# ReGLU feed-forward for 32 tokens: projections with the tokens as the stationary operand, and h transposed chunk by chunk

## The chip, the cores and the metric

The kernel runs on one core of a Trainium2 chip. The metric is the device time in microseconds. The kernel before takes 63.21 us, the median of 6 runs (62.99 to 63.34).

## The reference

```python
B, S, D, F = 32, 1, 1024, 3584          # x [32,1,1024], all bfloat16
def reference(x, W_gate, W_up, W_down):
    gate = jnp.einsum("bsd,df->bsf", x, W_gate)
    up = jnp.einsum("bsd,df->bsf", x, W_up)
    gate = gate * (lambda x, dt: x.astype(dt))(gate > 0, gate.dtype)   # Relu
    h = gate * up
    return jnp.einsum("bsf,fd->bsd", h, W_down)
```

There are only 32 tokens, but three weight matrices of 7.34 MB each, 22 MB together, and each weight is used once.

## The kernel before

All weights get a place in on-chip memory and are loaded once. x is loaded by ScalarE's DMA queue (L180), turned by eight TensorE transposes (L122) and copied to xT by ScalarE (L182): 128 partitions, KT = 8 slices of the model dimension, 32 tokens. Partition p holds rows 8p to 8p+7 of W_gate and W_up, so that slice kt is one row per partition.

The hidden dimension F = 3584 is split into NG = 7 groups of 512, each into J = 4 tiles of 128, so FT = 28 tiles. A projection tile (`proj_tiles`, L126 to L138) takes a 128x128 block of weights as the stationary operand and the 32 tokens of xT as the moving one, eight matmuls over kt, and leaves 128 hidden units (partitions) by 32 tokens in PSUM. 28 tiles times 8 slices make 224 matmuls with 224 weight loads, for gate and for up alike. In this orientation h comes out with hidden units on partitions, which is what the down projection needs as its stationary operand. ScalarE applies Relu to gate in two pieces (L184 for tiles 0 to 15, L188 for 16 to 27), and DVE multiplies by up, in the same two pieces (L201, L206), into hT.

The down projection (`down_tile`, L140 to L153) takes a 128x32 tile of hT as stationary and 128x512 of W_down as moving, two matmuls per tile for the two halves of the output, 56 in all, accumulating in o_ps. ScalarE copies the first half out of PSUM and sends it (L192, L194), DVE the second (L210), SyncE sends that (L113).

The order of work is written out by hand. SyncE's queue issues the loads in this order: Wg whole (L100), Wu for tiles 0 to 15 (L102, called WuA below), the Wd chunk g = 0 (L103), the rest of Wu (L105, WuB), Wd chunks 1 to 5 (L107), and the last Wd chunk in four quarters (L109), each with its own semaphore. TensorE follows that order: gate, up A, down chunk 0, up B, down chunks 1 to 6. Each matmul in the program is a pair of instructions for TensorE, a weight load and a matmul.

Of the kernel before, what the change touches and what calls it, by code (L numbers as in the profile page):

```python
# [5 lines left out]
ACT = mybir.ActivationFunctionType  # L6
ALU = mybir.AluOpType


def bass_standalone__glu_gated_reglu__sampling_kernel(  # L10
# [7 lines left out]
    bf16 = mybir.dt.bfloat16  # L18
    fp32 = mybir.dt.float32

    B, S, D = x.shape
    F = W_gate.shape[1]
    P = 128
    N = B * S
    KT = D // P
    GW = 4 * P
    NG = F // GW
    J = 4
    FT = NG * J
    DH = 512  # L30
    NDH = D // DH
    HALF_T = 16
    GA = HALF_T // J

    assert N <= P and D % P == 0 and F % GW == 0 and D % DH == 0
    assert FT > HALF_T

    x2 = x.flatten_outer_dims()
    out2 = out.flatten_outer_dims()
    Wg_v = W_gate.rearrange("(p kt) f -> p kt f", kt=KT)  # L40
    Wu_v = W_up.rearrange("(p kt) f -> p kt f", kt=KT)
    Wd_v = W_down.rearrange("(g q j) d -> q g j d", q=P, j=J)

    with ExitStack() as es:
        x_sb = es.enter_context(nc.sbuf_tensor("x_sb", [N, D], bf16))
        ident = es.enter_context(nc.sbuf_tensor("ident", [N, N], bf16))
        xT = es.enter_context(nc.sbuf_tensor("xT", [P, KT, N], bf16))
        Wg = es.enter_context(nc.sbuf_tensor("Wg", [P, KT, F], bf16))
        Wu = es.enter_context(nc.sbuf_tensor("Wu", [P, KT, F], bf16))
        Wd = es.enter_context(nc.sbuf_tensor("Wd", [P, NG, J, D], bf16))  # L50
        g_sb = es.enter_context(nc.sbuf_tensor("g_sb", [P, FT, N], fp32))
        hT = es.enter_context(nc.sbuf_tensor("hT", [P, FT, N], bf16))
        o_sb = es.enter_context(nc.sbuf_tensor("o_sb", [N, D], bf16))
        xT_ps = es.enter_context(nc.psum_tensor("xT_ps", [P, KT, N], bf16))
        g_ps = es.enter_context(nc.psum_tensor("g_ps", [P, FT, N], fp32))
        u_ps = es.enter_context(nc.psum_tensor("u_ps", [P, FT, N], fp32))
        o_ps = es.enter_context(nc.psum_tensor("o_ps", [N, D], fp32))

        sem = lambda name: es.enter_context(nc.semaphore(name))
        s_x = sem("s_x")  # L60
        s_ident = sem("s_ident")
        s_xT_ps = sem("s_xT_ps")
        s_xT = sem("s_xT")
        s_wg = sem("s_wg")
        s_wuA = sem("s_wuA")
        s_wuB = sem("s_wuB")
        s_wd = [sem(f"s_wd{g}") for g in range(NG - 1)]
        s_wd6 = [sem(f"s_wdl{j}") for j in range(J)]
        s_g = sem("s_g")
        s_u = sem("s_u")  # L70
        s_gr = sem("s_gr")
        s_h = sem("s_h")
        s_o = sem("s_o")
        s_osb0 = sem("s_osb0")
        s_osb1 = sem("s_osb1")
        s_out0 = sem("s_out0")
# [1 line left out]
        block = es.enter_context(nc.Block())  # L78

        x_v = x_sb[:, :].rearrange("b (p kt) -> b kt p", kt=KT)  # L80
        Wg_r = Wg[:, :, :].rearrange("p kt (g q j) -> p kt g j q", g=NG, j=J)
        Wu_r = Wu[:, :, :].rearrange("p kt (g q j) -> p kt g j q", g=NG, j=J)

        @block.gpsimd
        def _(pool):
# [11 lines left out]

        @block.sync
        def _(sp):
            sp.dma_start(Wg[:, :, :], Wg_v[:, :, :]).then_inc(s_wg, 16)  # L100
            fa = slice(0, GA * GW)
            sp.dma_start(Wu[:, :, fa], Wu_v[:, :, fa]).then_inc(s_wuA, 16)  # L102
            sp.dma_start(Wd[:, 0, :, :], Wd_v[:, 0, :, :]).then_inc(s_wd[0], 16)  # L103
            fb = slice(GA * GW, F)
            sp.dma_start(Wu[:, :, fb], Wu_v[:, :, fb]).then_inc(s_wuB, 16)  # L105
            for g in range(1, NG - 1):
                sp.dma_start(Wd[:, g, :, :], Wd_v[:, g, :, :]).then_inc(s_wd[g], 16)  # L107
            for j in range(J):
                sp.dma_start(Wd[:, NG - 1, j, :], Wd_v[:, NG - 1, j, :]).then_inc(  # L109
                    s_wd6[j], 16  # L110
                )
            sp.wait_ge(s_osb1, 1)
            sp.dma_start(out2[:, DH:D], o_sb[:, DH:D]).then_inc(s_out1, 16)  # L113
            sp.wait_ge(s_out1, 16)
            sp.wait_ge(s_out0, 16)

        @block.tensor
        def _(pe):
            pe.wait_ge(s_x, 16)
            pe.wait_ge(s_ident, 2)  # L120
            for kt in range(KT):
                ins = pe.transpose(xT_ps[:, kt, :], x_v[:, kt, :], ident[:, :])  # L122
            ins.then_inc(s_xT_ps, 1)
            pe.wait_ge(s_xT, 1)

            def proj_tiles(W_r, ps, t_lo, t_hi):  # L126
                ins = None
                for t in range(t_lo, t_hi):
                    g, j = divmod(t, J)
                    for kt in range(KT):  # L130
                        ins = pe.matmul(  # L131
                            ps[:, t, :],
                            W_r[:, kt, g, j, :],
                            xT[:, kt, :],
                            start=(kt == 0),
                            stop=(kt == KT - 1),
                        )
                return ins  # L138

            def down_tile(t):  # L140
                g, j = divmod(t, J)
                ins = []
                for h in range(NDH):
                    ins.append(
                        pe.matmul(  # L145
                            o_ps[:, h * DH : (h + 1) * DH],
                            hT[:, t, :],
                            Wd[:, g, j, h * DH : (h + 1) * DH],
                            start=(t == 0),
                            stop=(t == FT - 1),  # L150
                        )
                    )
                return ins  # L153

            pe.wait_ge(s_wg, 16)
            proj_tiles(Wg_r, g_ps, 0, HALF_T).then_inc(s_g, 1)
            proj_tiles(Wg_r, g_ps, HALF_T, FT).then_inc(s_g, 1)
            pe.wait_ge(s_wuA, 16)
            proj_tiles(Wu_r, u_ps, 0, HALF_T).then_inc(s_u, 1)
            pe.wait_ge(s_h, 1)  # L160
            pe.wait_ge(s_wd[0], 16)
            for j in range(J):
                down_tile(j)
            pe.wait_ge(s_wuB, 16)
            proj_tiles(Wu_r, u_ps, HALF_T, FT).then_inc(s_u, 1)
            for g in range(1, NG - 1):
                if g == GA:
                    pe.wait_ge(s_h, 2)
                pe.wait_ge(s_wd[g], 16)
                for j in range(J):  # L170
                    down_tile(g * J + j)
            for j in range(J):
                pe.wait_ge(s_wd6[j], 16)
                last = down_tile((NG - 1) * J + j)
            last[0].then_inc(s_o, 1)
            last[1].then_inc(s_o, 1)

        @block.scalar
        def _(act):
            act.dma_start(x_sb[:, :], x2[:, :]).then_inc(s_x, 16)  # L180
            act.wait_ge(s_xT_ps, 1)
            act.activation(xT[:, :, :], xT_ps[:, :, :], ACT.Copy).then_inc(s_xT, 1)  # L182
            act.wait_ge(s_g, 1)
            act.activation(  # L184
                g_sb[:, 0:HALF_T, :], g_ps[:, 0:HALF_T, :], ACT.Relu
            ).then_inc(s_gr, 1)
            act.wait_ge(s_g, 2)
            act.activation(  # L188
                g_sb[:, HALF_T:FT, :], g_ps[:, HALF_T:FT, :], ACT.Relu
            ).then_inc(s_gr, 1)  # L190
            act.wait_ge(s_o, 1)
            act.activation(o_sb[:, 0:DH], o_ps[:, 0:DH], ACT.Copy).then_inc(s_osb0, 1)  # L192
            act.wait_ge(s_osb0, 1)
            act.dma_start(out2[:, 0:DH], o_sb[:, 0:DH]).then_inc(s_out0, 16)  # L194
            act.wait_ge(s_out0, 16)

        @block.vector
        def _(dve):
            dve.wait_ge(s_gr, 1)
            dve.wait_ge(s_u, 1)  # L200
            dve.tensor_tensor(  # L201
                hT[:, 0:HALF_T, :], g_sb[:, 0:HALF_T, :], u_ps[:, 0:HALF_T, :], ALU.mult
            ).then_inc(s_h, 1)
            dve.wait_ge(s_gr, 2)
            dve.wait_ge(s_u, 2)
            dve.tensor_tensor(  # L206
                hT[:, HALF_T:FT, :], g_sb[:, HALF_T:FT, :], u_ps[:, HALF_T:FT, :], ALU.mult
            ).then_inc(s_h, 1)
            dve.wait_ge(s_o, 2)
            dve.tensor_copy(o_sb[:, DH:D], o_ps[:, DH:D]).then_inc(s_osb1, 1)  # L210


# [26 lines left out]
```

## Time and profile before

| | before |
|---|---|
| time, median of 6 runs | 63.21 us |
| profiled execution: time / span of the core | 63.24 / 61.4 us |
| TensorE matmul busy / weight load busy | 31.6 / 21.5 us (512 of each) |
| DVE, ScalarE busy | 1.9, 3.3 us |
| gate matmuls, 128x128 stationary, 32 moving | 224, 7.8 us busy |
| up matmuls, same shape | 224, 7.8 us busy |
| down matmuls, 128x32 stationary, 512 moving | 56, 15.4 us busy |
| bytes read from HBM | 22.09 MB, 361 GB/s over the span |
| mean granted TensorE clock | 0.889 |

The profile is of one execution. The span is the time from the first to the last instruction of the core; the execution's own time is 1.84 us longer. "PE" is TensorE's matmuls, "PEld" its weight loads, "ACT" ScalarE, "SP" SyncE, and "PEq", "SPq" are the sequencers. "<-" behind an idle time names what ended it. The busy time of a row is not its cost: matmuls overlap, so the distance between starts is what counts. The clock is the share of full speed that the chip grants TensorE.

### The profile page before, as it was taken

How to read it: one execution, taken by the hardware profiler on the slowest of the kernel's cores; microseconds unless marked ns; L12 is line 12 of the kernel's file. 1: busy time of each engine (PE TensorE's matmuls, PEld its weight loads, DVE VectorE, ACT ScalarE, POOL GpSimd, SP SyncE). 2: the span in 40 equal slices, each digit the busy share in tenths (PEclk: the TensorE clock that was granted, in tenths of full speed). 3: DMA queues.
4: the chain of work that ended last, by engine and by line, in shares of the span. 5: the costliest groups of instructions: out<-in, count | busy, mean ns of one | idle time of the engine just before them, and what ended most of it. 6: DMA issues, size and time to landing. Idle time of an engine off the chain costs nothing.

```text
span 61.4 us, 1089 instructions
## 1 busy us (share of the span) xinstructions
PE 31.6 (51%) x512; PEld 21.5 (35%) x512; DVE 1.9 (3%) x3; ACT 3.3 (5%) x5; POOL 0.5 (1%) x6
## 2 busy tenths in 40 slices
PE   0000004000000499992209985972999999769920
PEld 0000003000000599992209972302993443314400
DVE  0000000000000000000000003000003000000040
ACT  2500000200000000300300000000000000000030
POOL 3000000000000000000000000000000000000000
PEclk9999999999999999999955555569955999999999
DMA  0909985991991999999999999999999999992001
GB/s 0 597 43 576 619 373 224 597 597 75 523 597 69 411 416 413 403 411 397 429 423 381 399 400 402 397 429 422 427 421 416 416 405 416 396 380 109 11 0 43
DMA packets 3812, 22.22 MB, mean 362 GB/s; under 512 B 256, under 2 KB 320, under 8 KB 2912
## 3 DMA queue, kind: packets, MB, share of 16 engines
q1 hardware_dynamic: 3712, 22.05, 88.5%
q10 hardware_dynamic: 96, 0.10, 0.5%
q8 instruction: 4, 0.07, 0.4%
HBM read 22.09 MB, written 0.07 MB: 361 GB/s over the span
## 4 chain that ended last, share of the span: by engine, by line
SPq 54%; DMA 34%; PE 6%; DVE 1%; issue 1%
DMA Wd<-in_W_down_dram 34%; SPq L107 26%; SPq L103 22%; PE o_ps L145 6%; SPq L105 5%; DVE o_sb L210 1%; SPq L102 1%; SPq L100 1%
## 5 line engine op out<-in xcount | busy, mean ns | idle before, releaser
L145 PE MATMUL o_ps<-Wd,hT 128*32 128x512 bf16 x56 | 15.4, 435 | 1.9 <-DMA Wd<-in_W_down_dram 1.0
L131 PE MATMUL g_ps<-xT,Wg 128*128 128x32 bf16 x224 | 7.8, 190 | 11.1 <-DMA Wg<-in_W_gate_dram 10.0
L131 PEld LDWEIGHTS g_ps<-xT,Wg 128*128 128x128 bf16 x224 | 7.6, 118 | 11.3 <-issue 11.3
L131 PE MATMUL u_ps<-xT,Wu 128*128 128x32 bf16 x224 | 7.8, 190 | 4.1 <-DMA Wu<-in_W_up_dram 4.1
L131 PEld LDWEIGHTS u_ps<-xT,Wu 128*128 128x128 bf16 x224 | 7.6, 118 | 5.1 <-DMA Wu<-in_W_up_dram 5.1
L145 PEld LDWEIGHTS o_ps<-Wd,hT 128*32 128x32 bf16 x56 | 5.7, 107 | 10.3 <-issue 3.9
L122 PE MATMUL xT_ps<-ident,x_sb 32*128 32x32 bf16 x8 | 0.7, 220 | 10.1 <-DMA x_sb<-in_x_dram 10.1
L122 PEld LDWEIGHTS xT_ps<-ident,x_sb 32*128 32x128 bf16 x8 | 0.6, 163 | 10.1 <-DMA x_sb<-in_x_dram 10.1
L192 ACT ACTIVATE o_sb<-o_ps 32x512 bf16<-32x512 f32 x1 | 0.6, 586 | 28.4 <-PE o_ps L145 28.4
L201 DVE TENSOR_TENSOR hT<-g_sb,u_ps 128x512 bf16<-128x512 f32 x1 | 0.7, 689 | 36.7 <-PE u_ps L131 36.7
L184 ACT ACTIVATE g_sb<-g_ps 128x512 f32<-128x512 f32 x1 | 0.6, 597 | 14.0 <-PE g_ps L131 14.0
L182 ACT ACT_TABLE_LOAD x1 | 1.3, 1283 | 1.2 <-PEq L224 1.2
L210 DVE CAST o_sb<-o_ps 32x512 bf16<-32x512 f32 x1 | 0.7, 678 | 12.1 <-PE o_ps L145 12.1
L182 ACT ACTIVATE xT<-xT_ps 128x256 bf16<-128x256 bf16 x1 | 0.4, 383 | 8.3 <-PE xT_ps L122 8.3
L206 DVE TENSOR_TENSOR hT<-g_sb,u_ps 128x384 bf16<-128x384 f32 x1 | 0.6, 555 | 8.7 <-PE u_ps L131 8.7
L188 ACT ACTIVATE g_sb<-g_ps 128x384 f32<-128x384 f32 x1 | 0.5, 490 | 3.9 <-PE g_ps L131 3.9
L88 POOL TENSOR_SCALAR_AFFINE_SELECT ident<-ident 32x32 bf16<-32x32 bf16 x1 | 0.2, 202 | 0.2 <-POOL ident L86 0.2
L86 POOL MEMSET ident<- 32x32 bf16 x1 | 0.1, 114 | 0.3 <-POOLq L224 0.3
L224 POOL MEMSET const-float32-0.0<- 128x1 f32 x1 | 0.1, 99 | 0.2 <-issue 0.2
L224 POOL MEMSET const-float32-1.0<- 128x1 f32 x1 | 0.1, 99 | 0.0
L224 POOL MEMSET const-bfloat16-1.0<- 128x1 bf16 x1 | 0.1, 99 | 0.0
L224 POOL MEMSET const-uint8-127<- 128x1 uint8 x1 | 0.1, 99 | 0.0
## 6 DMA issues: line engine op xcount, KB each, us to landing
Wg<-in_W_gate_dram SPq DMA_DIRECT2D x1, 7168.0 KB, 19.9
Wd<-in_W_down_dram SPq DMA_DIRECT2D x6, 1024.0 KB, 20.2
Wu<-in_W_up_dram SPq DMA_DIRECT2D x1, 4096.0 KB, 31.0
Wu<-in_W_up_dram SPq DMA_DIRECT2D x1, 3072.0 KB, 27.2
Wd<-in_W_down_dram SPq DMA_DIRECT2D x4, 256.0 KB, 19.4
x_sb<-in_x_dram ACTq DMA_DIRECT2D x1, 64.0 KB, 9.3
out_dram<-o_sb ACTq DMA_DIRECT2D x1, 32.0 KB, 1.5
out_dram<-o_sb SPq DMA_DIRECT2D x1, 32.0 KB, 1.5
```

The costliest lines, as they stand in the source:

```text
L100: sp.dma_start(Wg[:, :, :], Wg_v[:, :, :]).then_inc(s_wg, 16)
L102: sp.dma_start(Wu[:, :, fa], Wu_v[:, :, fa]).then_inc(s_wuA, 16)
L103: sp.dma_start(Wd[:, 0, :, :], Wd_v[:, 0, :, :]).then_inc(s_wd[0], 16)
L105: sp.dma_start(Wu[:, :, fb], Wu_v[:, :, fb]).then_inc(s_wuB, 16)
L107: sp.dma_start(Wd[:, g, :, :], Wd_v[:, g, :, :]).then_inc(s_wd[g], 16)
L122: ins = pe.transpose(xT_ps[:, kt, :], x_v[:, kt, :], ident[:, :])
L131: ins = pe.matmul(ps[:, t, :], W_r[:, kt, g, j, :], xT[:, kt, :], start=(kt == 0), stop=(kt == KT - 1),)
L145: pe.matmul(o_ps[:, h * DH : (h + 1) * DH], hT[:, t, :], Wd[:, g, j, h * DH : (h + 1) * DH], start=(t == 0), stop=(t == FT - 1),)
L182: act.activation(xT[:, :, :], xT_ps[:, :, :], ACT.Copy).then_inc(s_xT, 1)
L184: act.activation(g_sb[:, 0:HALF_T, :], g_ps[:, 0:HALF_T, :], ACT.Relu).then_inc(s_gr, 1)
L201: dve.tensor_tensor(hT[:, 0:HALF_T, :], g_sb[:, 0:HALF_T, :], u_ps[:, 0:HALF_T, :], ALU.mult).then_inc(s_h, 1)
L210: dve.tensor_copy(o_sb[:, DH:D], o_ps[:, DH:D]).then_inc(s_osb1, 1)
```

## The change

The projections are turned round. For each slice kt the 128x32 slice of xT is the stationary operand and 128x512 of the weights the moving one; the result has 32 tokens on partitions and 512 hidden units in one PSUM bank. Seven banks (`acc`) hold all of F, and the loop over kt is now outside the loop over the seven chunks, so all seven accumulate at once. Wg and Wu are loaded in eight slices each, in the order of kt, each with a semaphore; all of Wu comes before all of Wd. Up reuses gate's banks, each once its Relu is done (`s_gr`).

Gate's Relu output and h now have tokens on partitions (`g_sb`, `h_sb`, bf16, in seven chunks). For the down projection, each chunk of h is turned by four TensorE transposes into PSUM (`tp`) and copied to hT by ScalarE. The transposes of chunk c+1 stand ahead of the down matmuls of chunk c. The down matmuls themselves, the Wd loads and the two output paths are as they were, except that the output accumulates in banks 0 and 1 of `acc`. SyncE no longer waits for the first output half (ScalarE still does).

```diff
-            sp.dma_start(Wg[:, :, :], Wg_v[:, :, :]).then_inc(s_wg, 16)
-            fa = slice(0, GA * GW)
-            sp.dma_start(Wu[:, :, fa], Wu_v[:, :, fa]).then_inc(s_wuA, 16)
-            sp.dma_start(Wd[:, 0, :, :], Wd_v[:, 0, :, :]).then_inc(s_wd[0], 16)
-            fb = slice(GA * GW, F)
-            sp.dma_start(Wu[:, :, fb], Wu_v[:, :, fb]).then_inc(s_wuB, 16)
-            for g in range(1, NG - 1):
-                sp.dma_start(Wd[:, g, :, :], Wd_v[:, g, :, :]).then_inc(s_wd[g], 16)
+            for kt in range(KT):
+                sp.dma_start(Wg[:, kt, :], Wg_v[:, kt, :]).then_inc(s_wg[kt], 16)
+            for kt in range(KT):
+                sp.dma_start(Wu[:, kt, :], Wu_v[:, kt, :]).then_inc(s_wu[kt], 16)
+            for c in range(NFC - 1):
+                sp.dma_start(Wd[:, c, :, :], Wd_v[:, c, :, :]).then_inc(s_wd[c], 16)
...
+            for kt in range(KT):
+                pe.wait_ge(s_wg[kt], 16)
+                for c in range(NFC):
+                    ins = pe.matmul(
+                        acc[:, c, :],
+                        xT[:, kt, :],
+                        Wg[:, kt, c * FC : (c + 1) * FC],
+                        start=(kt == 0),
+                        stop=(kt == KT - 1),
+                    )
+                    if kt == KT - 1:
+                        ins.then_inc(s_gc, 1)
+            for kt in range(KT):
+                pe.wait_ge(s_wu[kt], 16)
+                for c in range(NFC):
+                    if kt == 0:
+                        pe.wait_ge(s_gr, c + 1)
...
+            def transpose_chunk(c):
+                pe.wait_ge(s_h, c + 1)
+                if c > 0:
+                    pe.wait_ge(s_hT, c)
+                for j in range(J):
+                    ins = pe.transpose(tp_t[:, c * J + j, :], h_v[:, c, j, :], ident[:, :])
+                ins.then_inc(s_hTp, 1)
+
+            def down_chunk(c):
+                pe.wait_ge(s_hT, c + 1)
+                if c == 0:
+                    pe.wait_ge(s_h, NDH)
+                if c < NFC - 1:
+                    pe.wait_ge(s_wd[c], 16)
...
+            transpose_chunk(0)
+            for c in range(NFC):
+                if c + 1 < NFC:
+                    transpose_chunk(c + 1)
+                last = down_chunk(c)
+            for h in range(NDH):
+                last[h].then_inc(s_o, 1)
...
+            for c in range(NFC):
+                act.wait_ge(s_gc, c + 1)
+                act.activation(
+                    g_sb[:, c * FC : (c + 1) * FC], acc[:, c, :], ACT.Relu
+                ).then_inc(s_gr, 1)
+            for c in range(NFC):
+                act.wait_ge(s_hTp, c + 1)
+                act.activation(
+                    hT[:, c * J : (c + 1) * J, :], tp_t[:, c * J : (c + 1) * J, :], ACT.Copy
+                ).then_inc(s_hT, 1)
...
+            for c in range(NFC):
+                dve.wait_ge(s_gr, c + 1)
+                dve.wait_ge(s_uc, c + 1)
+                dve.tensor_tensor(
+                    h_sb[:, c * FC : (c + 1) * FC],
+                    g_sb[:, c * FC : (c + 1) * FC],
+                    acc[:, c, :],
+                    ALU.mult,
+                ).then_inc(s_h, 1)
```

More of the change, by code (lines that the diff above doesn't have):

```diff
@@ L25, in bass_standalone__glu_gated_reglu__sampling_kernel @@
     KT = D // P
[L26 to L29, printed above, removed]
+    FC = 512
+    NFC = F // FC
+    J = FC // P
+    FT = NFC * J
     DH = 512
     NDH = D // DH
[L32 to L36, printed above, removed]
+    assert N <= P and D % P == 0 and F % FC == 0 and D == NDH * DH and NDH <= 2
+    assert (KT + FT) * N * 2 <= 2048 or True
     x2 = x.flatten_outer_dims()
@@ L41, in bass_standalone__glu_gated_reglu__sampling_kernel @@
     Wu_v = W_up.rearrange("(p kt) f -> p kt f", kt=KT)
-    Wd_v = W_down.rearrange("(g q j) d -> q g j d", q=P, j=J)
+    Wd_v = W_down.rearrange("(c q j) d -> q c j d", q=P, j=J)
     with ExitStack() as es:
@@ L49, in bass_standalone__glu_gated_reglu__sampling_kernel @@
         Wu = es.enter_context(nc.sbuf_tensor("Wu", [P, KT, F], bf16))
-        Wd = es.enter_context(nc.sbuf_tensor("Wd", [P, NG, J, D], bf16))
-        g_sb = es.enter_context(nc.sbuf_tensor("g_sb", [P, FT, N], fp32))
+        Wd = es.enter_context(nc.sbuf_tensor("Wd", [P, NFC, J, D], bf16))
+        g_sb = es.enter_context(nc.sbuf_tensor("g_sb", [N, F], bf16))
+        h_sb = es.enter_context(nc.sbuf_tensor("h_sb", [N, F], bf16))
         hT = es.enter_context(nc.sbuf_tensor("hT", [P, FT, N], bf16))
         o_sb = es.enter_context(nc.sbuf_tensor("o_sb", [N, D], bf16))
[L54 to L57, printed above, removed]
+        acc = es.enter_context(nc.psum_tensor("acc", [N, NFC, FC], fp32))
+        tp = es.enter_context(nc.psum_tensor("tp", [P, 1024], bf16))
+        tp_t = tp[:, 0 : FT * N].rearrange("p (t b) -> p t b", b=N)
+        xT_ps = tp_t[:, 0:KT, :]
         sem = lambda name: es.enter_context(nc.semaphore(name))
@@ L63, in bass_standalone__glu_gated_reglu__sampling_kernel @@
         s_xT = sem("s_xT")
[L64 to L70, printed above, removed]
+        s_wg = [sem(f"s_wg{k}") for k in range(KT)]
+        s_wu = [sem(f"s_wu{k}") for k in range(KT)]
+        s_wd = [sem(f"s_wd{c}") for c in range(NFC - 1)]
+        s_wdl = [sem(f"s_wdl{j}") for j in range(J)]
+        s_gc = sem("s_gc")
         s_gr = sem("s_gr")
+        s_uc = sem("s_uc")
         s_h = sem("s_h")
+        s_hTp = sem("s_hTp")
+        s_hT = sem("s_hT")
         s_o = sem("s_o")
@@ L80, in bass_standalone__glu_gated_reglu__sampling_kernel @@
         x_v = x_sb[:, :].rearrange("b (p kt) -> b kt p", kt=KT)
-        Wg_r = Wg[:, :, :].rearrange("p kt (g q j) -> p kt g j q", g=NG, j=J)
-        Wu_r = Wu[:, :, :].rearrange("p kt (g q j) -> p kt g j q", g=NG, j=J)
+        h_v = h_sb[:, :].rearrange("b (c q j) -> b c j q", c=NFC, j=J)
         @block.gpsimd
@@ L99, in _ @@
         def _(sp):
-            sp.dma_start(Wg[:, :, :], Wg_v[:, :, :]).then_inc(s_wg, 16)
-            fa = slice(0, GA * GW)
-            sp.dma_start(Wu[:, :, fa], Wu_v[:, :, fa]).then_inc(s_wuA, 16)
-            sp.dma_start(Wd[:, 0, :, :], Wd_v[:, 0, :, :]).then_inc(s_wd[0], 16)
-            fb = slice(GA * GW, F)
-            sp.dma_start(Wu[:, :, fb], Wu_v[:, :, fb]).then_inc(s_wuB, 16)
-            for g in range(1, NG - 1):
-                sp.dma_start(Wd[:, g, :, :], Wd_v[:, g, :, :]).then_inc(s_wd[g], 16)
+            for kt in range(KT):
[4 more added lines that the diff above has]
+                sp.dma_start(Wd[:, c, :, :], Wd_v[:, c, :, :]).then_inc(s_wd[c], 16)
             for j in range(J):
-                sp.dma_start(Wd[:, NG - 1, j, :], Wd_v[:, NG - 1, j, :]).then_inc(
-                    s_wd6[j], 16
+                sp.dma_start(Wd[:, NFC - 1, j, :], Wd_v[:, NFC - 1, j, :]).then_inc(
+                    s_wdl[j], 16
                 )
@@ L114, in _ @@
             sp.wait_ge(s_out1, 16)
-            sp.wait_ge(s_out0, 16)
         @block.tensor
@@ L124, in _ @@
             pe.wait_ge(s_xT, 1)
[L126 to L136, printed above, removed]
-                        )
-                return ins
@@ L140, in down_tile @@
[L140 to L176, printed above, removed]
+            for kt in range(KT):
[10 more added lines that the diff above has]
+                        ins.then_inc(s_gc, 1)
@@ new lines, in _ @@
+            for kt in range(KT):
[3 more added lines that the diff above has]
+                        pe.wait_ge(s_gr, c + 1)
+                    ins = pe.matmul(
+                        acc[:, c, :],
+                        xT[:, kt, :],
+                        Wu[:, kt, c * FC : (c + 1) * FC],
+                        start=(kt == 0),
+                        stop=(kt == KT - 1),
+                    )
+                    if kt == KT - 1:
+                        ins.then_inc(s_uc, 1)
@@ new lines, in transpose_chunk @@
+            def transpose_chunk(c):
[11 more added lines that the diff above has]
+                    pe.wait_ge(s_wd[c], 16)
+                last = None
+                for j in range(J):
+                    t = c * J + j
+                    if c == NFC - 1:
+                        pe.wait_ge(s_wdl[j], 16)
+                    last = []
+                    for h in range(NDH):
+                        last.append(
+                            pe.matmul(
+                                acc[:, h, :],
+                                hT[:, t, :],
+                                Wd[:, c, j, h * DH : (h + 1) * DH],
+                                start=(t == 0),
+                                stop=(t == FT - 1),
+                            )
+                        )
+                return last
@@ L178, in _ @@
+            transpose_chunk(0)
[3 more added lines that the diff above has]
+                last = down_chunk(c)
+            for h in range(NDH):
+                last[h].then_inc(s_o, 1)
         @block.scalar
@@ L181, in _ @@
             act.wait_ge(s_xT_ps, 1)
[L182 to L190, printed above, removed]
+            act.activation(xT[:, :, :], xT_ps, ACT.Copy).then_inc(s_xT, 1)
+            for c in range(NFC):
[8 more added lines that the diff above has]
+                ).then_inc(s_hT, 1)
             act.wait_ge(s_o, 1)
-            act.activation(o_sb[:, 0:DH], o_ps[:, 0:DH], ACT.Copy).then_inc(s_osb0, 1)
+            act.activation(o_sb[:, 0:DH], acc[:, 0, :], ACT.Copy).then_inc(s_osb0, 1)
             act.wait_ge(s_osb0, 1)
@@ L198, in _ @@
         def _(dve):
[L199 to L210, printed above, removed]
+            for c in range(NFC):
[4 more added lines that the diff above has]
+                    g_sb[:, c * FC : (c + 1) * FC],
+                    acc[:, c, :],
+                    ALU.mult,
+                ).then_inc(s_h, 1)
+            if NDH > 1:
+                dve.wait_ge(s_o, NDH)
+                dve.tensor_copy(o_sb[:, DH:D], acc[:, 1, :]).then_inc(s_osb1, 1)
 _INS = ['x', 'W_gate', 'W_up', 'W_down']
```

## The prediction

> **What bounds the kernel now.** I read the chain that ended last in order of time first, then the tail of the DMA stream by windows, then the instruction queue and the one gap on TensorE that no wait explains, then the clock. The chain's last pieces (start, length, what):
>
> ```profile
> 34.35 20.76 DMA Wd<-in_W_down_dram
> 55.11 0.04 issue
> 55.15 3.64 PE o_ps L145 x16
> 58.80 0.02 issue
> 58.82 0.68 DVE o_sb L210
> ```
>
> What sets the end is the weight stream: the sixth of seven W_down chunks (g = 5) lands at 55.11, then 16 down matmuls (chunks 5 and 6) run without a pause, then DVE empties the second half and the output goes out (2.6 us from 58.80 to the span's end). TensorE is busy for half the span and is waiting for data at 55.11. So the first question is not what the matmuls cost, but when chunk 5 lands. Windows of the end (window, length, busy by engine, clock, DMA share, GB/s):
>
> ```profile
> 53.50:54.50 1.00, 1.00 (x6) 0.29 (x3) 0.00 (x0) 0.00 (x0) 0.00 (x0) 1.00 1.02 385
> 55.60:56.00 0.40, 0.40 (x3) 0.19 (x2) 0.00 (x0) 0.00 (x0) 0.00 (x0) 1.00 0.27 102
> 56.00:56.40 0.40, 0.40 (x3) 0.19 (x2) 0.00 (x0) 0.00 (x0) 0.00 (x0) 1.00 0.27 102
> ```
>
> The share falls to about 4 of 16 engines while 2 us of landings are still to come: four DMA engines lag. The semaphore increments in the trace say the same: for chunk 5, twelve engines report at 52.98 to 53.41 and four at 54.67 to 55.11; for the last quarter of chunk 6, 55.65 to 56.05 and 57.27 to 57.69. On Wg (20.0 to 20.6) no engine lags. One lags at the landing of WuA, three at WuB, four from chunk 4 on. What steps in between? Queue 8, and TensorE stopping with no releaser:
>
> ```profile
> q8 instruction: 4, 0.07, 0.4%
> 29.16 0.48 PE L131 MATMUL g_ps<-xT,Wg 128*128 128x32 bf16 x10 [1.14 <-issue]
> ```
>
> The four instruction packets start at 26.80, 32.84, 38.98 and 49.16, each 16 KB and 1.0 to 1.1 us long, and each new laggard appears in the first landing after one of them. Four packets, four lagging engines, each late by about 1.3 us: I take the lag to be TensorE's own instruction fetch, queued in front of weights on one engine each time. The first one even starves TensorE (28.0 to 29.16), after 449 instructions of TensorE are in the trace, of 1,032 in all.
>
> **What the change removes: the instructions.** Before, TensorE runs 512 pairs of load and matmul (1,024 rows). After: 8 pairs for xT, 7 chunks x 8 slices = 56 for gate, 56 for up, 28 for the h transposes, 56 for down: 204 pairs, 408 rows. Second waits on one instruction become instructions of their own; in this trace three stand between TensorE's matmuls. I count 16 after (one before gate, one before up, six in the transposes, eight in the down part). With start and end some 435, short of the 449 where the first fetch came. So no fetch should fall inside the stream, and all engines should land as the twelve did: chunk 5 by 53.41, 1.7 us earlier. [...]
>
> **The stream itself.** The bytes stay: 22.05 MB. Wg goes from 128 runs of 57,344 bytes to eight transfers with runs of 7,168; Wu from runs of 4,096 and 3,072 to 7,168; Wd is the same. From landings on the fast engines: WuA's 64 runs per engine take 10.21 us (160 ns each), WuB's 64 take 7.78 (122), a Wd chunk's 8 take 2.49 (311). A straight line through these (about 38 ns per KB and 8 ns per run) puts a 7,168 run at 273 ns and a slice (8 runs) at 2.19. Wu: 8 x 2.19 = 17.5 against 10.21 + 7.78 = 18.0, gain 0.5. Wg: its packets took 2.12 to 2.19 each, so 8 slices lose about 0.3. Net -0.2, with 0 to -0.5 as bounds. Chunk 5 then lands at 53.41 - 0.2 = 53.2. SyncE issues 26 loads where it issued 13; a Wg load with 128 runs took 0.38 us to issue against 2.19 to move, so the issue stays ahead and costs nothing; if it fell behind, every slice would be late by the difference. The x load now shares with 7 KB packets and not 57 KB ones, where it took 9.3 us; its wait is hidden either way until slice 0 lands at about 20.5 - 7 x 2.19 = 5.2.
>
> **Gate and up on TensorE.** Each matmul now has the shape of L145: 128 rows, 32 stationary columns, 512 moving. In the window at clock 0.50, weight loads of L145 start 0.43 us apart; at 1.00 the last 16 start (58.4 - 55.15)/15 = 0.217 apart. A slice is seven: 1.52 us at full clock, 3.0 at half, against 2.19 between landings. At full clock it hides, with 0.7 us idle per slice; at half it doesn't. The clock in the trace:
>
> ```profile
> 30.80:41.00 10.20, 7.96 (x136) 5.37 (x136) 0.69 (x1) 0.00 (x0) 0.00 (x0) 0.50 1.02 401
> 41.00:44.40 3.40, 1.81 (x53) 1.74 (x53) 0.00 (x0) 0.00 (x0) 0.00 (x0) 0.99 1.03 426
> 47.90:61.40 13.50, 9.85 (x44) 3.92 (x42) 0.68 (x1) 0.59 (x1) 0.00 (x0) 1.00 0.61 239
> ```
>
> (Before 27.4 us the trace holds no clock record, so I don't count the page's nines there.) It changes in steps of 3.41 us. It rose at 41.0 and 47.9, each time in a stretch that ended in unbroken 512-column matmuls; it fell after a stretch with 53% busy in 32-column matmuls; it held from 47.9 on with gaps of 0.5 us. [...] If every slice ran at half clock: 16 x 3.0 from 5.2 gives 53, then 7 x 3.7 of down part gives 79, in all some 83 us. But a TensorE that is behind is never idle, and the rows show that unbroken 512-column work brings the clock up within about one step. One half-clock step of 3.41 us does 3.41/3.0 = 1.1 slices while 1.6 arrive, a lag of 0.5 slice or 0.7 us, which full clock works off in one to two slices. So gate ends about 1.6 us after slice 7 (20.5) and up about 1.7 after slice 15 (38.0). In between, the first up matmul of each bank waits for its Relu: seven of 0.59 us (L192's 32x512 row) from 21.0 end at 25.1, and all later up matmuls queue behind. Slice 9 lands at 24.9, so this costs at most 0.3 and is made up.
>
> **The new chain to h.** DVE multiplies seven chunks (0.68 each, by L210's 32x512 row, the nearest) from 38.4; chunk 0 is done at 39.2, chunk 1 at 39.9. Four transposes like L122's (eight in 0.68) are 0.3 us; ScalarE's copy of 128x128 is about 0.28 (L182, L188 and L184: 0.38, 0.49, 0.60 for 256, 384, 512). Down chunk 0 wants chunk 1's transposes first, so it is ready at about 40.4; its weights land at 38.0 + 2.5 = 40.5. Hidden, by 0.1 us; if the cover goes, the delay is worked off: a chunk is 8 x 0.217 + 0.3 = 2.04 us at full clock against 2.49 between landings. Transposes of chunk c+1 stand ahead of down chunk c in TensorE's queue, but their h and copy were finished a chunk earlier. At half clock a chunk is 3.7, one such step lags 0.9 us, worked off in two to three chunks.
>
> **The sum.** Chunk 5 at 53.2 instead of 55.11, and TensorE idle by then (chunk 4 lands near 50.7, done at 52.8). Then the same 16 matmuls, 3.64 (the last quarter lands at about 55.85, and is wanted at 56.2), the same copy and output. The span becomes 61.4 - 1.9 = 59.5; the profiled execution took 63.24, 1.84 outside the span, and stands 0.03 above the median of 63.21. Forecast: 59.5 + 1.84 = 61.3.
>
> **The rivals.** (1) Fetching stays: a fetch is triggered early, or the four laggards have another cause. Then chunk 5 lands near 54.9 and only the 0.2 from run length is left: 63.0. For it: my margin is 14 instructions in 449, and later fetches came after other counts (about 510, 735, 960). Against: the first came exactly when TensorE ran dry. Chance 0.15. (2) Slower: the clock is at half when the tail begins. The wait for chunk 0 near 40 us, or the 20% slack per chunk, lets it fall, and the 16 last matmuls, which nothing covers, cost 0.43 each: +3.4, so 64.8. It decides once 9 of the 16 are at half clock (9 x 0.213 = 1.9, the whole gain). For it: a fall at 53% busy. Against: a hold at 83% (51.3 to 54.7), and the tail's approach is some 80% busy with 512-column work, nearer to that; bounds for the tail are 0 and +3.4, I take 0. Chance 0.17, whole or in part. (3) Half clock nearly throughout, 83 us: 0.01. The forecast case keeps 0.67, by itself 60.9 to 61.8.
>
> **How the numbers follow.** The low end is the stream gaining 0.5 and not 0.2, with a tail slightly shorter: 60.9. The high end takes in rival 1 and the mild part of rival 2: 63.4, leaving out about 0.15. A difference of 0.3% (0.2 us) is what this kernel's runs can tell. Faster: the main case, half of rival 1 (63.0 lies on the edge) and a little of rival 2: 0.76; same: 0.08; slower: 0.16.
>
> **What would show it.** Right: no packet on the instruction queue inside the stream, all 16 engines together in the last windows, chunk 5 landing near 53.2, clock 1.00 over the last 16 matmuls, idle of about 0.7 us per slice on TensorE in gate and up. Wrong: four or any engines still lagging (rival 1), the end windows at 0.50 (rival 2), slices landing more than 2.3 us apart, or a down part in which TensorE never waits for Wd.

## The result and the profile after

The changed kernel takes 62.94 us (median of 10 runs, 62.66 to 63.07) against 63.21 (20 runs): ratio 0.9945, 95% interval 0.9918 to 0.9972. It is faster, by 0.27 us between the medians where 1.9 was forecast. Three of e2's ten executions (63.70 to 64.01 us) fell into a slower state and are left out of its median and ratio below. The profiled execution took 62.83 us with a span of 61.0 (before: 63.24 and 61.4). What I had as the first rival, with 63.0, is what came.

The end of the chain, in order of time, has the shape it had:

```profile
52.23 1.89 PE acc L171 x8
54.12 0.25 PE tp L154 x4
54.39 0.29 ACT hT L201
54.67 0.12 issue
54.80 3.63 PE acc L171 x16
58.45 0.68 DVE o_sb L223
```

The same 16 matmuls, 3.63 us as before, now start at 54.80 and not at 55.15. The chain names ScalarE's copy as what came ahead of them. That is a trap: the copy at 54.39 belongs to chunk 6, and chunk 5's own had been done at 52.2. The trace shows 16 landings for each load, which I take as one from each of the 16 DMA engines, and TensorE waits for all 16. The last one of W_down chunk 5 came at 54.66, and TensorE started 0.14 later, as it did at chunks 1 to 4 (chunk 1: landed 44.64, started 44.77). The weights still set the end.

The instruction queue, and the windows of the end beside those shown of before (queue: packets, MB, share of the 16 engines; windows in the columns of the prediction):

```profile
q8 instruction: 1, 0.02, 0.1%
```

```profile
53.50:54.50 1.00, 0.85 (x7) 0.30 (x5) 0.00 (x0) 0.11 (x1) 0.00 (x0) 1.00 1.06 393
55.60:56.00 0.40, 0.40 (x4) 0.19 (x2) 0.00 (x0) 0.00 (x0) 0.00 (x0) 1.00 0.07 26
56.00:56.40 0.40, 0.40 (x4) 0.19 (x2) 0.00 (x0) 0.00 (x0) 0.00 (x0) 1.00 0.07 26
```

One packet where there were four, and a DMA share of 0.07, one engine of 16, where 0.27 stood. So with fewer instructions there are three laggards fewer. But TensorE's wait is for all 16 landings. Chunk 5 reports from fifteen engines at 52.81 to 53.32 and from the last at 54.66. The packet starts at 33.28, and TensorE shows when it hit (the last line is cut off by the window's end):

```profile
31.89 1.68 PE L139 MATMUL acc<-Wu,xT 128*32 128x512 bf16 x7 [0.50 <-DMA Wu<-in_W_up_dram]
35.50 1.69 PE L139 MATMUL acc<-Wu,xT 128*32 128x512 bf16 x7 [1.93 <-DMA Wu<-in_W_up_dram]
37.52 0.82 PE L139 MATMUL acc<-Wu,xT 128*32 128x512 bf16 x3 [0.33 <-DMA Wu<-in_W_up_dram]
```

Starts come every 2.18 us until 31.89. The next slice comes 3.6 us later, then the old rhythm returns and the delay stays to the end.

### The profile page after: what moved, and what is told of

The parts are those of the page before. It is cut to its first block, busy times and chain, and to the rows that moved or that the text cites. A ratio compares the mean times of both kernels' runs of the same rounds, so it can differ in the third digit from the quotient of the medians.

```text
span 61.0 us, 519 instructions
## 1 busy us (share of the span) xinstructions
PE 44.5 (73%) x204; PEld 17.3 (28%) x204; DVE 4.9 (8%) x8; ACT 7.7 (13%) x17; POOL 0.5 (1%) x6
## 4 chain that ended last, share of the span: by engine, by line
DMA 42%; PE 27%; SPq 20%; ACT 2%; DVE 2%; issue 2%
DMA Wu<-in_W_up_dram 42%; PE acc L171 21%; SPq L102 14%; SPq L100 6%; PE acc L139 3%; PE tp L154 2%; ACT hT L201 2%; DVE o_sb L223 1%; DVE h_sb L215 1%
## 5 line engine op out<-in xcount | busy, mean ns | idle before, releaser
L139 PE MATMUL acc<-Wu,xT 128*32 128x512 bf16 x56 | 13.8, 381 | 4.9 <-DMA Wu<-in_W_up_dram 4.8
L125 PE MATMUL acc<-Wg,xT 128*32 128x512 bf16 x56 | 15.4, 431 | 2.3 <-DMA Wg<-in_W_gate_dram 2.3
L171 PE MATMUL acc<-Wd,hT 128*32 128x512 bf16 x56 | 13.1, 379 | 1.9 <-ACT hT L201 1.9
L125 PEld LDWEIGHTS acc<-Wg,xT 128*32 128x32 bf16 x56 | 5.6, 106 | 11.7 <-DMA Wg<-in_W_gate_dram 3.5
L139 PEld LDWEIGHTS acc<-Wu,xT 128*32 128x32 bf16 x56 | 4.7, 96 | 14.0 <-DMA Wu<-in_W_up_dram 8.6
L215 DVE TENSOR_TENSOR h_sb<-g_sb,acc 32x512 bf16<-32x512 bf16 x7 | 4.3, 669 | 40.2 <-PE acc L139 40.2
L171 PEld LDWEIGHTS acc<-Wd,hT 128*32 128x32 bf16 x56 | 5.0, 96 | 7.5 <-ACT hT L201 2.2
L196 ACT ACTIVATE g_sb<-acc 32x512 bf16<-32x512 f32 x7 | 3.5, 580 | 16.0 <-PE acc L125 16.0
L201 ACT ACTIVATE hT<-tp 128x128 bf16<-128x128 bf16 x7 | 1.9, 277 | 27.9 <-PE tp L154 27.9
L154 PE MATMUL tp<-ident,h_sb 32*128 32x32 bf16 x28 | 2.1, 184 | 0.5 <-DVE h_sb L215 0.5
```

The lines of the kernel that those rows point to most:

```text
L125: ins = pe.matmul(acc[:, c, :], xT[:, kt, :], Wg[:, kt, c * FC : (c + 1) * FC], start=(kt == 0), stop=(kt == KT - 1),)
L139: ins = pe.matmul(acc[:, c, :], xT[:, kt, :], Wu[:, kt, c * FC : (c + 1) * FC], start=(kt == 0), stop=(kt == KT - 1),)
L154: ins = pe.transpose(tp_t[:, c * J + j, :], h_v[:, c, j, :], ident[:, :])
L171: pe.matmul(acc[:, h, :], hT[:, t, :], Wd[:, c, j, h * DH : (h + 1) * DH], start=(t == 0), stop=(t == FT - 1),)
L196: act.activation(g_sb[:, c * FC : (c + 1) * FC], acc[:, c, :], ACT.Relu).then_inc(s_gr, 1)
L201: act.activation(hT[:, c * J : (c + 1) * J, :], tp_t[:, c * J : (c + 1) * J, :], ACT.Copy).then_inc(s_hT, 1)
```

## The experiments

Two theories. A: TensorE's code fetch delays one DMA engine by about 1.3 us, once per packet on the instruction queue; the first packet is asked for when about 200 instructions have been passed, not 449 (in the changed kernel 203 of TensorE's rows in the trace start before the packet). B: the lag belongs to the stream and the packet only coincides with it. All kernels are edits of the changed one, except e8. Each ratio is to the kernel before on the same chip.

**e1, little code.** Gate and up run only the last slice, one transpose per chunk is done, and down chunks 0 and 1 use one tile: arithmetic is left out, all loads stay.

```diff
-            for kt in range(KT):
+            for kt in range(KT - 1, KT):
...
-                for j in range(J):
+                for j in range(1):
...
-                for j in range(J):
+                for j in range(1 if c < 2 else J):
```

> All loads as in the changed kernel, but TensorE's program is cut to 174 instructions: gate and up use only the last slice, one transpose per chunk, down chunks 0 and 1 only their first tile (arithmetic is left out). Theory A (TensorE's code fetch delays one DMA engine by 1.3 us; the first fetch comes when about 200 instructions have been passed): no packet on the instruction queue, all 16 engines land chunk 5 together by 53.3 to 53.5, the 16 last matmuls start about 1.3 us earlier than in the changed kernel, time 61.6. Theory B (the laggard has another cause, in the stream itself): one engine still lands chunk 5 about 1.3 us late, time 62.9. If the clock is at half in the tail, up to 3.4 is added in either case and the landings decide.

Measured: 61.90 us (4 runs, 61.48 to 62.31), ratio 0.981 (0.976 to 0.987, with the 95% interval in brackets here and below). The list of queues has no instruction row at all, and the windows of the end drain to nothing:

```profile
q1 hardware_dynamic: 3792, 22.05, 89.3%
q10 hardware_dynamic: 96, 0.10, 0.5%
```

```profile
55.60:56.00 0.40, 0.40 (x4) 0.16 (x3) 0.00 (x0) 0.00 (x0) 0.00 (x0) 1.00 0.01 5
56.00:56.40 0.40, 0.40 (x3) 0.18 (x2) 0.00 (x0) 0.00 (x0) 0.00 (x0) 1.00 0.00 0
```

All 16 engines land chunk 5 at 52.74 to 53.57. The profiled execution (62.31) started its 16 matmuls only at 54.3, because TensorE, idle for most of the run, worked on chunk 2 with starts 0.43 us apart, the step that before has at clock 0.50, and was late; so this run doesn't show the full gain.

**e2, the same little work with more code.** e1 with 100 needless transposes in front, 374 instructions.

```diff
+            for _ in range(100):
+                pe.transpose(tp_t[:, KT, :], x_v[:, 0, :], ident[:, :])
             for kt in range(KT):
                 ins = pe.transpose(xT_ps[:, kt, :], x_v[:, kt, :], ident[:, :])
```

> The short kernel (same arithmetic left out) with 100 needless small transposes ahead of the x transposes: 374 instructions. Theory A: one packet on the instruction queue, now early (5 to 15 us, right after instruction 200), one engine late by 1.3 us from then on, chunk 5 complete at about 54.7, time about 62.9. Theory B: the padding changes nothing against the short kernel, whatever that shows.

Measured: 62.92 us (7 runs, 62.55 to 63.35), ratio 0.998 (0.994 to 1.002). One packet, at 12.20, after 219 of TensorE's rows. One engine late from there: chunk 5 from fifteen engines by 53.22, complete at 54.55.

```profile
q8 instruction: 1, 0.02, 0.1%
```

```profile
56.00:56.40 0.40, 0.40 (x3) 0.17 (x2) 0.00 (x0) 0.00 (x0) 0.00 (x0) 1.00 0.07 26
```

```profile
28.56 25.99 DMA Wd<-in_W_down_dram
54.55 0.14 issue
54.69 3.63 PE acc L173 x16
```

The two programs differ in nothing but instructions whose result is not used and that are done by 11 us. Chunk 5 is complete 1.0 us later in e2 (53.57 to 54.55), and the time is 1.0 us longer (61.90 to 62.92), with no execution of one within the range of the other. B falls: the packet moved from 33 to 12 us with the code, and without the code there is no laggard.

**e9 and e5, more fetches.** Does each fetch cost, or only the worst engine? e9 is the changed kernel with e2's padding (636 instructions).

> The changed kernel with 100 needless small transposes at the start only, where TensorE has slack: 636 instructions, arithmetic unchanged. Padding takes 6.2 us, gate starts at 10.6 with three slices waiting, caught up by about 22, so TensorE should be on time at chunk 5 (it was not with padding in every slice). Theory A: two packets on the instruction queue (early, and near 43 us), two engines late by 1.3 us, chunk 5 complete at 54.6 to 55.1, time 62.8 to 63.0, the same as with one packet. Rival, each fetch costs time of its own: 63.4 to 64.2.

Measured: 62.83 us (12 runs), ratio 0.995 (0.992 to 0.998); the unpadded kernel, e7, is 62.78, 0.994. Two packets (12.34 and 45.67; the second was expected near 43), two late engines (54.55 and 54.66), so chunk 5 complete at 54.66:

```profile
q8 instruction: 2, 0.03, 0.2%
```

```profile
55.60:56.00 0.40, 0.40 (x4) 0.19 (x2) 0.00 (x0) 0.00 (x0) 0.00 (x0) 1.00 0.13 51
```

Two engines of 16 (0.13) instead of one (0.07), and no time lost that these runs can tell. The first late engine costs 1.0 us (e1 against e2), the second nothing. e5 was meant to show the same with three fetches, with 64 transposes in front and 8 behind each slice:

```diff
                     if kt == KT - 1:
                         ins.then_inc(s_gc, 1)
+                pad(8)
```

> The changed kernel with needless small transposes (64 at the start, 8 after each slice of gate and up): 820 instructions for TensorE instead of 436, arithmetic unchanged. [...]

Measured: 66.8 us (4 runs), 4.0 above e7, which I had not expected, and my mistake: 8 transposes take 0.6 us, so a slice costs TensorE 2.21 us against 2.18 between landings, and the late start is never made up (gate begins at 9.3, 3.7 after its first slice landed, and loses more over its first two slices, for the most part with starts 0.43 us apart). Up ends at 47 and not at 41, and the down part runs without a pause. The landings do answer the question: packets at 13.5, 35.0 and 56.1, after 183, 458 and 742 rows, and chunk 5 complete at 54.68 with the two late engines that it then had. The time says nothing on the fetch.

**e4, one load each for Wg and Wu.** What is the slicing worth in this orientation?

```diff
-            for kt in range(KT):
-                sp.dma_start(Wg[:, kt, :], Wg_v[:, kt, :]).then_inc(s_wg[kt], 16)
+            sp.dma_start(Wg[:, :, :], Wg_v[:, :, :]).then_inc(s_wg[0], 16)
```

> The changed kernel with Wg in one transfer and Wu in one, each waited for once. If the slices are what hides the 512-column matmuls: gate can start at 20.9 and up only at about 39, 56 matmuls of 0.217 plus a cold start end at 52 to 54, seven down chunks of 2.04 behind them at 66 to 69, time 71 to 73. Rival, the stream alone sets the time: 63.

Measured: 70.73 us (one run). Gate, up and down by line:

```profile
L139 PE MATMUL acc<-Wu,xT 128*32 128x512 bf16 x56 | 13.9, 413 | 3.1 <-DMA Wu<-in_W_up_dram 3.1
L124 PE MATMUL acc<-Wg,xT 128*32 128x512 bf16 x56 | 13.8, 411 | 10.0 <-DMA Wg<-in_W_gate_dram 10.0
L171 PE MATMUL acc<-Wd,hT 128*32 128x512 bf16 x56 | 13.1, 380 | 0.0
```

The down part's idle time is 0.0: from gate on TensorE is the bound, but for the 3.1 us that up waits for Wu, with some 41 us of matmuls that can't start before 20.7. That is the cover that the slices give, some 8 us of time by this one run.

**e3, e6, e8 and e7: the tail.** Whatever lands late, 16 matmuls stand behind chunk 5, because it is waited for as one megabyte. e3 loads chunk 5 in quarters too, and TensorE waits for each, e6 also splits the last quarter in two; e8 is e3's edit in the kernel before; e7 repeats the changed kernel beside them.

```diff
-            for c in range(NFC - 1):
+            for c in range(NFC - 2):
                 sp.dma_start(Wd[:, c, :, :], Wd_v[:, c, :, :]).then_inc(s_wd[c], 16)
-            for j in range(J):
...
+            for i in range(2 * J):
+                c, j = NFC - 2 + i // J, i % J
+                sp.dma_start(Wd[:, c, j, :], Wd_v[:, c, j, :]).then_inc(s_wdl[i], 16)
```

> The changed kernel, with W_down chunk 5 also loaded and waited for in four quarters. If the tail is the 16 matmuls behind one landing: TensorE now follows the quarters and ends 0.6 after the last one lands (57.2 + 0.2 for shorter runs): end at 58.0 to 58.2 instead of 58.4, time 62.5 to 62.7. Rival: the extra waits and the shorter runs eat it: 62.9 to 63.1.

> As the kernel with chunk 5 in quarters, and the last quarter of chunk 6 loaded and waited for in two halves of the output width. Only one matmul then stands behind the last landing: about 0.2 us less than the quarters, less 0.1 for runs of 1,024 bytes: 62.2 to 62.4. Rival, the shorter runs and one more wait eat it: 62.4 to 62.6.

> The kernel before with chunk 5 also in quarters. If the 16 matmuls behind chunk 5 are a cost of the load size and not of the orientation: TensorE ends 0.6 after the last landing (57.7 + 0.2), at 58.4 instead of 58.8, time 62.8 to 62.9. Rival, in the old order TensorE is behind at the end anyway and gains nothing: 63.1 to 63.2.

> The changed kernel itself, beside the others on one chip: 62.8 to 63.0, one packet on the instruction queue.

| | us (runs) | ratio to before | 95% interval |
|---|---|---|---|
| e7, changed | 62.78 (12) | 0.994 | 0.992 to 0.996 |
| e3, chunk 5 in quarters | 62.41 (6) | 0.990 | 0.986 to 0.993 |
| e6, and last quarter in halves | 62.29 (6) | 0.988 | 0.984 to 0.992 |
| e8, before with quarters | 62.90 (12) | 0.997 | 0.994 to 1.000 |

The end of e3's chain:

```profile
54.06 0.23 PE tp L153 x4
54.29 3.69 PE acc L170 x16
58.01 0.68 DVE o_sb L222
```

The 16 matmuls start at 54.29, before the last quarter of chunk 5 is in (54.75), and end 0.45 earlier than in the changed kernel, 0.65 behind the last landing at 57.32. Both e3 and e6 are faster than both kernels: their slowest executions (62.53, 62.52) stay below e7's fastest (62.63). e6 ran on e7's chip, e3 on another, where the kernel before took the same 63.09. Between e3 and e6 the intervals don't decide. e8's interval touches 1, so for the old order this stays inconclusive; its profile ends the last matmul at 58.53 (58.4 was expected) instead of 58.79.

## Why the prediction was wrong, point by point

**The step that failed: "With start and end some 435, short of the 449 where the first fetch came. So no fetch should fall inside the stream".** The count was right (the trace has 428 rows for TensorE, and the built program 436 instructions). The threshold was wrong. 449 is where TensorE ran dry, not where its code was asked for. "The first came exactly when TensorE ran dry" misread the trace of before: the packet starts at 26.80, after 385 rows, and TensorE stops only at 28.0. By 385 alone, 435 instructions would have called for a fetch.

In the other runs the first packet starts after 203 rows in the changed kernel (and in e3, e6 and e7), 219, 225, 183, 172 and 365 in e2, e9, e5, e4 and e8, and never in e1, which has 174 instructions. The number of packets goes up with the instructions: none at 174, one at 374 and 436, two at 636, three at 820, four in before (1,032 rows). Later packets start after 501 rows in e9 and 458 and 742 in e5, so 276, 275 and 284 rows behind the packet before them, where before has 124, 225 and 222. For 385 in before (and 365 in e8) a delay may stand behind the count: the gate part there runs some 61 rows per us. Take row 193, a mark of my choosing. It started at 23.6, 3.2 us ahead of the packet, and in those 3.2 us some 190 more rows ran. In the changed kernel TensorE runs 6 to 7 rows per us; row 193 started at 32.1, 1.2 us ahead of the packet, ten rows. That is a reading and not shown, since in e4 and e5 the packet comes before row 193. But I could have doubted 449 from before alone: its packets at rows 385, 509, 734 and 956 have no even step, and I noted the later counts under the rival and kept 449.

**The mechanism was right.** Fetches make the laggards: four and four before, one and one after, none in e1, two in e9. What the forecast didn't work out is what one fetch leaves: the lag is a maximum and not a sum. From four to one gains next to nothing; only from one to none pays. With none, e1 has chunk 5 complete at 53.57, near the forecast's 53.2. In the changed kernel it was complete 0.45 us earlier than before (55.11 to 54.66): 0.09 on the engines that are on time (53.41 to 53.32), the rest because the lag of the last one behind them was 1.34 and not 1.70. I take that to be which of the engines, spread over 0.4 us among themselves, were hit; no run tells it. So most of the 0.27 us has no shown cause: it came again in e7, but it is not the gain that was forecast, and that the change came out faster at all is luck as far as the runs show. TensorE gave 0.1 back: it started 0.14 after the landing, where it had been 0.04.

**The stream.** A slice at 2.19: measured 2.18. Chunk 5 at 53.2 on all engines: 53.32 on fifteen. The net gain from longer runs was put at 0.2 and is 0.09 or less.

**Gate and up.** Starts 0.43 us apart at first (to 10.4, where the trace has no clock record yet) and 0.217 at clock 1.00 were right, and the idle per slice shows as 0.50 (the rows' ends are longer than the step of starts). TensorE was busy without a pause from 5.76, and the clock's first record in the trace is full speed from 10.7 on, held past the last matmul. Windows of gate, up and down:

```profile
10.70:20.50 9.80, 8.75 (x38) 3.24 (x36) 0.00 (x0) 0.00 (x0) 0.00 (x0) 1.00 1.01 420
25.30:33.50 8.20, 6.67 (x28) 2.38 (x28) 0.00 (x0) 0.00 (x0) 0.00 (x0) 1.00 1.02 421
44.70:54.70 10.00, 8.47 (x48) 3.63 (x48) 0.00 (x0) 1.15 (x5) 0.00 (x0) 1.00 1.01 412
```

So rival 2 (half clock in the tail) did not come; two more executions had a mean granted clock of 0.97 and took 62.90 and 62.98, within the range of the rest. In gate and up nine waits of 0.3 to 0.5 us and one of 1.93 after 10.7 us left the clock at 1.00. The fall that the prediction read in before, at 44.5, came without longer waits: TensorE's longest in the 3.41 us ahead of it was 1.59 us, before the matmul at 42.66. What brought it about, no run shows.

**The chain to h.** DVE's row took 0.67 (0.68 forecast), the copy 0.28, four transposes 0.30. Down chunk 0 started at 42.29, 0.13 after its weights (42.16), when chunk 1's transposes were just done too, so the cover was used up; chunk 1 was on time again.

**The tail.** 3.64 forecast, 3.63 measured, and the 2.6 us behind it unchanged.

## What to carry to other kernels

TensorE's wait for a load ended with the last of 16 landings (54.66 for chunk 5, with fifteen in by 53.32), so count who is late and by how much: removing three of four equal delays gained almost nothing here, removing the last one 1.0 us. When a count of instructions is read as a trigger, check it against a second event at another instruction rate, since a delay in time can look like a different count. And before trimming what works on a stream that keeps the DMA engines full (share 1.01 to 1.02 here), look at how much work waits behind its last landings: smaller last pieces gained 0.4 us here, the change itself 0.3.

## What the runs showed of the hardware

One 16 KB fetch of TensorE's code took 1.0 to 1.1 us on one DMA engine (1.2 in e5's third) and set that engine back by about 1.3 us (1.34 at chunk 5 in the changed kernel), more than the 0.6 to 0.7 us that 16 KB of weights take it (a quarter chunk, 256 KB in 16 landings, lands every 0.62 to 0.68 us). The engine did not catch up: in e2 it is 1.27 behind the next at 15.5 us and 1.24 at 57.1. By the number of late engines at chunk 5 (four for four packets in before, one for one in the changed kernel, two for two in e9), the packets of a run each hit another engine.

The moment of the packet isn't settled: against the start of row 193 it comes 3.2 us later in before, 2.2 in e2, 2.3 in e9, 1.2 in the changed kernel, and 2.0 and 2.4 us earlier in e5 and e4. Whether one row sets it off, which one, and how far ahead of its execution, stays open. A full kernel without any fetch wasn't tried: the pairs that the change needs alone are 408 instructions. So the 1.0 us stands for a kernel with most of its arithmetic left out.
